# Token lists of a routed expert layer: running ranks and a step function over partitions instead of one-hot products

## The chip, the cores and the metric

The kernel runs on one core of one Trainium2 chip. The metric is the device time of one execution in microseconds; the median over repeated runs counts. TensorE is called PE here, VectorE DVE, ScalarE ACT, GpSimd POOL and SyncE SP.

## What is computed

The reference chains three layers. With `x` of 8 x 3072 x 256:

```python
X = np.fft.fft(np.fft.fft(x, axis=1), axis=2).real      # 24576 tokens of 256
g = X @ w_gate
y = (g / (1 + np.exp(-g)) * (X @ w_val)) @ w_out        # 1536 hidden columns
logits = y @ moe2_w_gate                                # 8 experts
# pairs (token, expert) in falling order of logit: a token takes the first expert
# that isn't full; an expert is full with 24576 / 8 = 3072 tokens
for e in range(8):
    mask = assigned == e
    out[mask] = np.maximum(y[mask] @ w1[e], 0) @ w2[e]  # 1024 hidden columns
```

The order of the pairs matters only through who gets which expert, so the kernel need not sort: it finds the expert that fills next and the logit at which it is full, gives it its tokens, shuts it, and goes on with the rest.

## The kernel before

**Phase 1** (`phase1`, L87 to L707) computes y and the logits. It has 48 tiles of 512 tokens (six to a batch), and 12 steps to a tile, one for 128 hidden columns. In a step PE makes the gate and value products (L385) and, for the step three earlier, the out products (L416), each in three passes over high and low parts. ACT and POOL split the hidden values into `hi` (L691) and `lo` (L692), DVE does the work between. POOL also folds the next batch's x (L120 to L134) and splits the transformed data (L371). What happens beside the steps is put into half steps by hand (`at`, `advance`). At a tile's end `finish` (L418) runs four times: ACT copies 128 rows of y and logits out of the accumulator (L423), POOL copies the eight logits to `Lall` (L424), and SP stores the 256 columns of y to `yscr` in DRAM. A tile's 128 rows are 128 tokens two apart, so the store goes to every second row of `yscr`; two columns of the first tile of a batch need one more small store each (L433).

**Phase 2** (`phase2`, L795 on) has eight rounds, one for each expert, in the order in which they fill.

*Search* (`search`, L841): the best open expert of each token (`choose`, L773: DVE), then eleven steps of three bits each that find the threshold. A step compares all logits with seven edges (L864, DVE), counts by products (L872, PE), picks out the counts (L876 to L880, DVE), sums them over partitions (L884, PE) and derives the next edges (L897 to L927, DVE). Then DVE marks the expert's tokens, and running sums along the 192 columns (L976) with products over the partitions (L982, L983) give each token its place in the list, 0 to 3071. POOL writes the logits of the next round, with the expert shut (`ml`, L964).

*Listing* (`listing`, L1007): place s is held as (s >> 7, s & 127). For 16 columns of tokens at a time DVE makes a one-hot matrix of the low part (`lo`, L1025, 128 x 2048), one of the high part (L1019), and the latter times the two bytes of the token's number (L1022). 192 products (L1014) of `lo[:, :, c]` with 48 columns add up the list, and two DVE operations (L1034, L1036) turn it into row numbers `idx`.

*Experts* (`up` L1087, `down` L1114): six blocks of 512 tokens. POOL gathers rows of y by `idx` with four indirect DMAs (L1062), PE transposes them (L1075), eight `up`s of six products (L1095) and four `down`s of 24 products (L1121) follow, and POOL scatters the result by `idx` (L1130). `split_w` (L1050) splits a quarter of an expert's weights: ACT casts (L1055), POOL subtracts (L1056).

*Order.* The program writes each engine's order out by hand. The first search and the first list run alone. After that the generators `searches` and `lists` run beside the products: `go(time)` (L1173) is called in 32 slots of each block, adds the slot's time to a credit (1.3 at most), and takes one step of the list and one of the search as long as the credit is positive; each step yields its cost in DVE time. A list may begin when its search is through and the expert before the current one is done. If the next list is not ready when an expert's last `up` is issued, slots are called with nothing between them until it is (L1206, L1207).

Of the kernel before, what the change touches and what calls it, by code (L numbers as in the profile page):

```python
# [12 lines left out]
I32 = mybir.dt.int32  # L13
AF = mybir.ActivationFunctionType
# [3 lines left out]
P = 128  # L18
# [39 lines left out]
def _tables():  # L58
    """The constant matrices of the two transforms."""
# [27 lines left out]
def phase1(ctx, tc, io, yscr, Lall, ident, NT, choice=None):  # L87
# [11 lines left out]
    # ---- the tables, and x of a batch  # L99
# [16 lines left out]
    def fold(b, i, xs, eng, tags=(("fa", 1), ("fb", 1))):  # L116
        """The sums and differences over the mirrors of both axes; takes two half steps an operation."""
# [24 lines left out]
    def fold_special(b, eng, tags=(("fa", 1), ("fb", 1))):  # L142
# [7 lines left out]
        # row s=768 of the odd sine transform takes the place of row s=0, which is zero  # L150
# [30 lines left out]
    # the words of a block of weights lie where its split parts come to lie  # L181
# [21 lines left out]
    def fold_w(j, gv, cs, tag, bufs):  # L203
        """Yields between the product and what reads it."""
# [56 lines left out]
    # ---- the column d=128, all batches at once  # L261
# [41 lines left out]
    # ---- the transform over s for a tile of 256 pairs: columns [k=1536-h-2j, j falling | k=2j+h]  # L303
    def fft_mm(pp, z, zsp, h, q, sine):
# [3 lines left out]
        if h == 0:  # L308
# [34 lines left out]
    def fft_half(t, sine, tb, res, bk=("F", 1)):  # L343
        """The cosine or the sine transform of a tile; yields before each part."""
# [3 lines left out]
        # the sine data of even k are those of B-, the cosine data of even k those of B+  # L348
# [25 lines left out]
    # ---- gate and value products, silu, out product  # L374
    order = ((0, 0), (1, 0), (0, 1))  # (weights, data) hi or lo
# [12 lines left out]
    def columns(g):  # L388
        """G = cosine part minus sine part, and their sum, mirrored, for the columns of the negative d."""
# [19 lines left out]
    def out_proj(g):  # L409
# [4 lines left out]
        for u in range(4):  # L414
            for i, (a, d) in enumerate(((0, 0), (0, 1), (1, 0))):  # h, weights
                nc.tensor.matmul(Yp[t][u], h[a][:, u * P : (u + 1) * P], Wo[c // 2][:, c % 2, d, :], start=(c == 0 and i == 0), stop=(c == NF - 1 and i == 2))  # L416

    def finish(t, u):  # L418
        b, hf, q = t // 6, (t // 3) % 2, t % 3
        base = b * S  # L420
# [3 lines left out]
        nc.gpsimd.tensor_copy(Lall[:, 4 * t + u, :], ys[:, D:EXT])  # L424
        # tokens of this column of the tile, by partition
        first = tokens(t, u)
        lo, hi = 0, P
        if hf == 0 and q == 0:
            # k=768 has the place of k=1536, which mini_tile() writes; k=0 is its own mirror
            lo, hi = ((0, P - 1), (0, P), (0, P - 1), (1, P))[u]  # L430
            if u == 0 or u == 3:
                k, r = ((base + 768, P - 1), (base + 2304, 0))[u // 3]
                nc.sync.dma_start(yscr[k : k + 1, :], ys[r : r + 1, 0:D])  # L433
        nc.sync.dma_start(yscr[first + 2 * lo : first + 2 * hi - 1 : 2, :], ys[lo:hi, 0:D])

    # ---- the rows k=1536 of all batches: their own mirrors
    def mini_tile():
        """Products in the second half of a step, what reads them in the first half of the next."""
# [52 lines left out]
        nc.sync.dma_start(yscr[1536 : N : S, :], ys[:, 0:D])  # L491
        nc.sync.dma_start(Lall[P - 1 : P, 2 : 4 * NT : 24, :], ys[:, D:EXT])
# [119 lines left out]
    def prep_block(j):  # L612
        """The last third of the weights during the first steps."""
# [49 lines left out]
    def finale():  # L663
        """The choice among the experts, beside the last products."""
# [45 lines left out]
def tokens(t, u):  # L710
    """The first of the 128 tokens, two apart, of column u of tile t."""
# [7 lines left out]
SHIFTS = tuple(range(29, 1, -3)) + (0,)  # the radix search: three bits at a time, the last time two  # L719
MOST = 1.3  # of the time of the vector engine, as much may be saved up  # L720
# [74 lines left out]
def phase2(ctx, tc, io, yscr, Lall, ident, first, out):  # L795
# [211 lines left out]
    def listing(res, first=False):  # L1007
# [9 lines left out]
        for a in range(0, NCOL, CB):  # L1017
# [9 lines left out]
            if todo:  # L1027
                products(*todo.pop())
# [250 lines left out]
```

## Time and profile before

| | |
|---|---|
| median of 3 runs | 3401.03 us (3399.63 to 3402.3) |
| span of the profiled execution | 3402.1 us, 66033 instructions |
| PE busy | 3243.1 us (95%) |
| DVE busy | 2667.1 us (78%) |
| POOL busy | 1833.1 us (54%) |
| ACT busy | 1559.9 us (46%) |
| mean granted clock of PE | 0.971 |

The page shows one execution; what lies around its span isn't shown apart. Busy times are unions of instructions. Products are pipelined, so a single product's duration holds its latency, and the pace of a row of products is read from their starts. Of a wait for several things the one that came last is named.

### The profile page before, as it was taken

How to read it: one execution, taken by the hardware profiler on the slowest of the kernel's cores; microseconds unless marked ns; L12 is line 12 of the kernel's file. 1: busy time of each engine (PE TensorE's matmuls, PEld its weight loads, DVE VectorE, ACT ScalarE, POOL GpSimd, SP SyncE). 2: the span in 40 equal slices, each digit the busy share in tenths (PEclk: the TensorE clock that was granted, in tenths of full speed). 3: DMA queues.
4: the chain of work that ended last, by engine and by line, in shares of the span. 5: the costliest groups of instructions: out<-in, count | busy, mean ns of one | idle time of the engine just before them, and what ended most of it. 6: DMA issues, size and time to landing. Idle time of an engine off the chain costs nothing.

```text
span 3402.1 us, 66033 instructions
## 1 busy us (share of the span) xinstructions
PE 3243.1 (95%) x25155; PEld 3065.6 (90%) x25155; DVE 2667.1 (78%) x5310; ACT 1559.9 (46%) x3022; POOL 1833.1 (54%) x1916
## 2 busy tenths in 40 slices
PE   5999999999999999999999749999999999999998
PEld 3899999999999999999999638888888888889998
DVE  7899999999999999999988877757666666677221
ACT  3556555655655556555655303232333232323343
POOL 4574664755746648557444344444445454545453
PEclk7999999999999999999999859999999999999999
DMA  5110100101001011010000001111111111111111
GB/s 197 30 36 22 50 23 31 48 17 42 31 29 48 17 31 48 17 42 31 23 17 17 17 31 43 52 41 53 44 57 44 57 45 55 40 60 60 43 47 36
DMA packets 72988, 141.83 MB, mean 42 GB/s; under 512 B 15266, under 2 KB 48978, under 8 KB 70624
## 3 DMA queue, kind: packets, MB, share of 16 engines
q1 hardware_dynamic: 51924, 70.46, 6.4%
q0 software_dynamic: 20736, 67.13, 5.9%
q8 instruction: 199, 3.26, 0.4%
q14 instruction: 117, 0.96, 0.1%
q10 hardware_dynamic: 12, 0.01, 0.0%
HBM read 87.17 MB, written 50.39 MB: 40 GB/s over the span
## 4 chain that ended last, share of the span: by engine, by line
PE 86%; DVE 7%; issue 3%; POOL 2%; ACT 1%; DMA 1%; SPq 0%; ACTq 0%; POOLq 0%; DVEq 0%
PE Y L416 22%; PE B L1121 16%; PE A L1095 14%; PE Q L385 11%; PE Pp L385 10%; PE L L1014 4%; PE F L325 2%; PE F L328 2%; PE C L872 2%; PE A L1075 1%; DVE T L396 1%; DVE lo L1025 1%; POOL lo L692 1%; DVE ise L969 1%; DVE hl L1112 1%
## 5 line engine op out<-in xcount | busy, mean ns | idle before, releaser
L692 POOL TENSOR_TENSOR lo<-hh,hi 128x512 fp32r<-128x512 f32 x576 | 746.0, 1295 | 707.0 <-ACT hi L691 696.0
L416 PE MATMUL Y<-Wo,hi 128*128 128x264 f32 x4608 | 866.8, 285 | 0.0
L416 PEld LDWEIGHTS Y<-Wo,hi 128*128 128x128 f32 x4608 | 710.6, 188 | 0.2 <-ACT hi L691 0.2
L416 PE MATMUL Y<-Wo,lo 128*128 128x264 f32 x2304 | 655.0, 284 | 4.5 <-POOL lo L692 3.5
L396 DVE SCALAR_TENSOR_TENSOR T<-tb,w,Q 128x256 f32<-128x256 f32 x1152 | 500.8, 475 | 118.8 <-ACT qs L685 112.1
L1121 PE MATMUL B<-w,hh 128*128 128x256 f32 x3072 | 584.1, 290 | 0.0
L685 ACT COPY qs<-Q 128x512 f32<-128x512 f32 x576 | 340.0, 590 | 520.6 <-PE Q L385 515.4
L1095 PE MATMUL A<-yh,w 128*128 128x512 f32 x1536 | 498.8, 406 | 15.4 <-DVE hl L1112 15.2
L1130 POOL DMA_INDIRECT out_dram<-ot,idx x192 | 201.3, 1048 | 547.6 <-ACT ot L1128 474.1
L1121 PEld LDWEIGHTS B<-w,hh 128*128 128x128 f32 x3072 | 481.0, 192 | 3.1
L404 DVE TENSOR_TENSOR hh<-sl,G 128x512 f32<-128x512 f32 x576 | 471.9, 819 | 1.3 <-ACT sl L699 1.3
L385 PE MATMUL Q<-xh,W 128*128 128x256 f32 x2304 | 445.8, 286 | 16.4 <-DVE T L396 8.3
L1112 DVE SCALAR_TENSOR_TENSOR hl<-A,hh 128x512 fp32r<-128x512 f32 x384 | 262.5, 686 | 243.5 <-ACT hh L1101 223.1
L416 PEld LDWEIGHTS Y<-Wo,lo 128*128 128x128 f32 x2304 | 434.4, 189 | 6.8 <-POOL lo L692 6.8
L1121 PE MATMUL B<-w,hl 128*128 128x256 f32 x1536 | 435.0, 283 | 2.8 <-DVE hl L1112 2.8
L385 PE MATMUL Pp<-xh,W 128*128 128x256 f32 x2304 | 431.1, 280 | 0.0
L1101 ACT ACTIVATE hh<-A 128x512 fp32r<-128x512 f32 x384 | 229.7, 598 | 405.1 <-PE A L1095 349.3
L397 DVE TENSOR_TENSOR G<-Pp,qs 128x512 f32<-128x512 f32 x576 | 392.2, 681 | 0.0
L691 ACT CAST hi<-hh 128x512 fp32r<-128x512 f32 x576 | 360.5, 626 | 65.8 <-DVE hh L404 62.0
L398 DVE TENSOR_TENSOR G<-T,Pp 128x512 f32<-128x512 f32 x576 | 389.1, 675 | 0.0
L385 PEld LDWEIGHTS Q<-xh,W 128*128 128x128 f32 x2304 | 354.3, 189 | 25.9 <-ACT hi L691 17.4
L699 ACT ACTIVATE sl<-G 128x512 f32<-128x512 f32 x576 | 365.4, 634 | 0.0
(241 smaller groups left out, 5653.7 us busy)
## 6 DMA issues: line engine op xcount, KB each, us to landing
xs<-in_x_dram SPq DMA_DIRECT2D x43, 512.0 KB
yscr<-ys SPq DMA_DIRECT2D x168, 128.0 KB
tb<-tscr SPq DMA_DIRECT2D x48, 128.0 KB
raw<-in_wg_dram SPq DMA_DIRECT2D x6, 512.0 KB
raw<-in_wv_dram SPq DMA_DIRECT2D x6, 512.0 KB
rawWo<-in_wo_dram SPq DMA_DIRECT2D x12, 256.0 KB
yg<-yscr,idx POOLq DMA_INDIRECT x192
out_dram<-ot,idx POOLq DMA_INDIRECT x192
```

Of the source, the lines that this page charges most:

```text
L385: nc.tensor.matmul(pp[:, gv * 256 : gv * 256 + 256], W[:, cs, gv, a, cc : cc + P], RI[t][cs][d], start=(i == 0), stop=(i == 2))
L396: nc.vector.scalar_tensor_tensor(T[:, gv, :], tb, w2[:, gv, c : c + 1], pq[:, gv * 256 : gv * 256 + 256], op0=ALU.mult, op1=ALU.add)
L397: nc.vector.tensor_sub(G[:, 0, :], pp, qs)
L398: nc.vector.tensor_add(rev(G[:, 1, :])[:, :, ::-1], T, rev(pp))
L404: nc.vector.tensor_mul(hh, s["sl"], s["G"][:, :, 256:512])
L416: nc.tensor.matmul(Yp[t][u], h[a][:, u * P : (u + 1) * P], Wo[c // 2][:, c % 2, d, :], start=(c == 0 and i == 0), stop=(c == NF - 1 and i ...
L685: nc.scalar.copy(s["qs"], s["pq"])
L691: nc.scalar.copy(hi, s["hh"])
L692: nc.gpsimd.tensor_sub(lo, s["hh"], hi.bitcast(F32))
L699: nc.scalar.activation(s["sl"], s["G"][:, :, 0:256], AF.Silu)
L1095: nc.tensor.matmul(pa, w[:, a, c : c + P], res["y", i][d][:, k, :], start=(n == 0), stop=(n == 5))
L1121: nc.tensor.matmul(pb[:, 0:D], h[a][:, s * P : (s + 1) * P], w[:, d, (f % 2) * D : (f % 2) * D + D], start=(n == 0), stop=(n == 23))
```

## The change

Three things change. In `finish` the row of y is stored whole, 264 columns, to the rows of `yscr` that the tile's partitions stand for, with the token's number (from a table of 16-bit integers) written over the first logit by POOL. In the search's end the marks are counted by the operations that make them, a running sum over the tokens at the threshold decides which of them still fit, and one more running sum gives `rank`, the number of the expert's tokens in a partition up to a column. The list is then made without one-hot matrices: products with a difference matrix give `x`, for each partition its ranks less those of the partition before, with the partition's start; a step function `on` (is place s at or after the start of partition p, 128 x 3072) summed with `x` over the partitions gives, for each place, the ranks of the partition in which it lies; and counting how many of them are at most the place's offset gives its column. The row number is column x 128 + partition. The scatter uses the token's number out of the gathered row. In the first round `close` (the logits of the next round) and the splits of the first expert's weights change their places in the order.

```diff
     def finish(t, u):
...
-        nc.gpsimd.tensor_copy(Lall[:, 4 * t + u, :], ys[:, D:EXT])
...
-                nc.sync.dma_start(yscr[k : k + 1, :], ys[r : r + 1, 0:D])
-        nc.sync.dma_start(yscr[first + 2 * lo : first + 2 * hi - 1 : 2, :], ys[lo:hi, 0:D])
+        c = 4 * t + u
+        nc.gpsimd.tensor_copy(Lall[:, c, :], ys[:, D:EXT])
+        nc.gpsimd.tensor_copy(ys[:, D : D + 1].bitcast(I32), idt[:, c : c + 1])
+        n = P - 1 if hf == 0 and q == 0 and u == 2 else P
+        nc.sync.dma_start(yscr[c * P : c * P + n, :], ys[0:n, :])
...
     nc.sync.dma_start(t["small"], io["cst"][:, 0:NSMALL])
+    nc.sync.dma_start(t["idt"], io["idt"])
...
+    sio = const.tile([P, CAP], I16, name="sio")
+    nc.sync.dma_start(sio, io["sio"].broadcast_to([P, CAP]))
-    iok = const.tile([P, P, CB], BF16, name="iok")
-    nc.scalar.copy(iok, along(prow, CB))
+    xrow = [const.tile([P, XW], BF16, name=f"xrow{i}") for i in range(2)]
...
-            ml = rp.tile([P, NCOL, E], F32, tag="ml", name="ml")
-            nc.gpsimd.tensor_add(ml, Lall, across(pen, NCOL))
-            res["next"] = ml
+            if ph > 0:
+                close(res)
         yield 1.2
...
         for k, op in enumerate((ALU.is_gt, ALU.is_equal)):
-            nc.vector.scalar_tensor_tensor(sel[:, k, :], m, thr, ise, op, ALU.mult)
-        yield 1.0
-        for k in range(2):
-            nc.vector.tensor_tensor_scan(sc[:, k, :], onesf, sel[:, k, :], 0.0, ALU.mult, ALU.add)
+            nc.vector.scalar_tensor_tensor(sel[:, k, :], m, thr, ise, op, ALU.mult, accum_out=num[:, k : k + 1])
         tot = rp.tile([P, 2], BF16, tag="tot", name="tot")
-        nc.vector.tensor_copy(tot, sc[:, :, NCOL - 1])
-        yield 0.7
-        yield from wait(3)
+        nc.vector.tensor_copy(tot, num)
+        yield 1.3
+        sc = rp.tile([P, NCOL], F32, tag="sc", name="sc")
+        nc.vector.tensor_tensor_scan(sc, onesf, sel[:, 1, :], -float(CAP), ALU.mult, ALU.add)
+        yield 0.4
+        yield from wait(2)
...
+        room = rp.tile([P, 1], F32, tag="room", name="room")
+        nc.vector.tensor_scalar(room, off[:, 1:2], off[:, 2:3], -1.0, ALU.add, ALU.mult)
+        fin = rp.tile([P, NCOL], F32, tag="fin", name="fin")
+        nc.vector.scalar_tensor_tensor(fin, sc, room, sel[:, 1, :], ALU.is_le, ALU.mult)
+        nc.vector.tensor_add(fin, fin, sel[:, 0, :])
+        yield 1.2
+        rank = rp.tile([P, NCOL], BF16, tag="rank", bufs=2, name="rank")
+        nc.vector.tensor_tensor_scan(rank, onesf, fin, 0.0, ALU.mult, ALU.add)
+        res["rank"] = rank
         if ph < E - 1:
-            nc.vector.scalar_tensor_tensor(alive, slot, 0.5, alive, ALU.is_lt, ALU.mult)
+            nc.vector.tensor_sub(alive, alive, fin)
+        yield 0.8
...
+    def listing(ph, res, first=None):
+        rank = res["rank"]
+        pd = bank("R", 1)
+        nc.tensor.matmul(pd[:, NCOL + 2 : NCOL + 3], trib, rank[:, NCOL - 1 : NCOL], start=True, stop=True)
+        nc.tensor.matmul(pd[:, NCOL : NCOL + 1], shiftb, rank[:, NCOL - 1 : NCOL], start=True, stop=True)
+        nc.tensor.matmul(pd[:, 0:NCOL], difb, rank, start=True, stop=True)
         yield 0
+        begin = rp.tile([P, 1], F32, tag="begin", name="begin")
+        nc.vector.tensor_copy(begin, pd[:, NCOL + 2 : NCOL + 3])
+        x = xrow[ph % 2]
+        nc.scalar.copy(x[:, 0 : NCOL + 1], pd[:, 0 : NCOL + 1])
+        yield 0.2
+        on = rp.tile([P, NS, P], BF16, tag="on", name="on")
+        flat = on.rearrange("p n s -> p (n s)")
+        for a in range(0, CAP, 512):
+            nc.vector.tensor_scalar(flat[:, a : a + 512], sio[:, a : a + 512], begin, None, ALU.is_ge)
+            yield 0.3
+        res["idx"] = []
+        for i in range(NS // 2):
+            pl = bank("A", 3) if first else bank("L", 1)
+            v = pl.rearrange("p (a c) -> p a c", a=2)
+            for a in range(2):
+                nc.tensor.matmul(v[:, a, 0:XW], on[:, 2 * i + a, :], x, start=True, stop=True)
+            yield 0
+            j = rp.tile([P, 2], F32, tag="j", bufs=2, name="j")
+            nc.vector.tensor_sub(j, siota[:, 2 * i : 2 * i + 2], v[:, :, NCOL])
+            cc = rp.tile([P, 2], F32, tag="cc", bufs=2, name="cc")
+            for a in range(2):
+                le = rp.tile([P, NCOL], F32, tag="le", bufs=2, name="le")
+                nc.vector.tensor_scalar(le, v[:, a, 0:NCOL], j[:, a : a + 1], None, ALU.is_le, ALU.add, accum_out=cc[:, a : a + 1])
...
+            nc.vector.scalar_tensor_tensor(res["idx"][-1][:, k : k + 2], cc, float(P), v[:, :, NCOL + 1], ALU.mult, ALU.add)
+            if first and i % 2:
+                first(i // 2)
+            yield 1.5
...
     def gather(res, i):
-        yg = work.tile([P, 4, D], F32, tag="yg", bufs=2, name="yg")
+        yg = work.tile([P, 4, EXT], F32, tag="yg", bufs=2, name="yg")
...
+        if k == 1:
+            res["id", i] = work.tile([P, 4], I32, tag="id", bufs=3, name="id")
+            nc.scalar.copy(res["id", i], yg[:, :, D].bitcast(I32))
...
     for _ in search(0, exp[0]):
         pass
-    for j, _ in enumerate(listing(exp[0], True)):
-        if j > 3 and j % 2 and j < 14:
-            split_w(exp[0], 1 + (j > 11))
-    gather(exp[0], 0)
-    for _ in range(3):
+    for _ in range(4):
+        split_w(exp[0], 1)
+
+    def begin(i):
+        if i == 0:
+            gather(exp[0], 0)
+            close(exp[0])
+
+    for _ in listing(0, exp[0], begin):
+        pass
+    for _ in range(4):
         split_w(exp[0], 2)
```

`NS` is 24 (blocks of 128 places) and `XW` is 194. `bank(tag, n)` takes the next of n accumulator banks, so `bank("L", 1)` waits for the readers of the pair before.

## Rows read from the trace of the kernel before

**Rows 1.** The page: the chain that ended last, by engine and by line.

```profile
PE 86%; DVE 7%; issue 3%; POOL 2%; ACT 1%; DMA 1%; SPq 0%; ACTq 0%; POOLq 0%; DVEq 0%
PE Y L416 22%; PE B L1121 16%; PE A L1095 14%; PE Q L385 11%; PE Pp L385 10%; PE L L1014 4%; PE F L325 2%; PE F L328 2%; PE C L872 2%; PE A L1075 1%; DVE T L396 1%; DVE lo L1025 1%; POOL lo L692 1%; DVE ise L969 1%; DVE hl L1112 1%
```

**Rows 2.** Windows by stage: us, busy PE, PEld, DVE, ACT, POOL; clock; DMA.

```profile
60.00:1860.00 1800.00, 1772.88 (x14664) 1750.76 (x14663) 1640.12 (x3076) 1052.02 (x2078) 1102.00 (x1082) 0.99 0.10 31
...
1925.00:2039.00 114.00, 43.62 (x351) 35.13 (x351) 90.98 (x221) 8.81 (x17) 37.83 (x35) 0.51 0.09 31
...
2219.00:3255.00 1036.00, 1019.06 (x7345) 909.64 (x7344) 662.45 (x1486) 337.51 (x625) 492.88 (x570) 0.99 0.15 50
```

**Rows 3.** Windows of expert 1 (list and search beside it) and 6 (list alone).

```profile
2218.00:2394.00 176.00, 172.63 (x1253) 152.93 (x1252) 119.66 (x277) 56.21 (x104) 83.04 (x97) 0.99 0.15 49
...
3095.00:3254.00 159.00, 159.00 (x1107) 146.49 (x1106) 64.36 (x106) 56.18 (x104) 78.73 (x94) 1.00 0.16 54
```

**Rows 4.** Line L1014 alone in the window of expert 1: busy PE, PEld.

```profile
2218.00:2394.00 176.00, 20.81 (x192) 18.26 (x192) 0.99 0.15 49
```

**Rows 5.** Instruction groups by line, whole span: the one-hot matrices on DVE.

```profile
L1025 DVE TENSOR_TENSOR lo<-hlb,iok 128x2048 bf16<-128x2048 bf16 x96 | 141.4, 1473 | 70.6 <-PE L L1014 70.3
...
L1022 DVE TENSOR_TENSOR v<-hi,idb 128x384 bf16<-128x384 bf16 x180 | 57.0, 355 | 3.3
```

**Rows 6.** Timeline around the first list: start us, duration us, instruction.

```profile
1986.51 3.43 POOL L964 TENSOR_TENSOR ml<-Lall,pen 128x1536 f32<-128x1536 f32 x1
...
1989.90 2.18 ACT L1055 CAST w<-w1f 128x512 fp32r<-128x512 f32 x4 [55.51 <-issue]
...
2030.56 0.18 DVE L1036 SCALAR_TENSOR_TENSOR idx<-L,idl 128x24 int32<-128x24 f32 x1
...
2034.81 0.95 POOL L1062 DMA_INDIRECT yg<-yscr,idx  x1 [0.30 <-issue]
...
2037.60 1.33 PE L1075 MATMUL A<-ident,yg 128*128 128x128 f32 x5 [0.74 <-DMA yg<-yscr,idx]
...
2038.75 1.22 PE L1095 MATMUL A<-yh,w 128*128 128x512 f32 x2
```

**Rows 7.** Instruction groups by line: operations like those of a pair, on DVE.

```profile
L995 DVE TENSOR_SCALAR si<-slot 128x192 int32<-128x192 f32 x8 | 2.1, 260 | 0.3
...
L900 DVE DVE_READ_ACCUMULATOR sat<-mx 128x1 f32 x70 | 5.8, 83 | 0.0
```

**Rows 8.** Timeline of PE in expert 1: products of a search step, the next.

```profile
2223.10 0.42 PE L872 MATMUL C<-ge,oh 128*128 128x112 bf16 x5
2223.34 0.70 PE L1095 MATMUL A<-yh,w 128*128 128x512 f32 x2
```

**Rows 9.** Waits of PE in the window of expert 1: total us, times, longest.

```profile
PE A L1095 <- DVE hl L1112: 3.1, 2, 2.8
```

**Rows 10.** Copies to Lall (min/median/max ns); timeline at tile ends; SP's start.

```profile
L424 POOL COPY Lall<-ys x189: 179/190/691, 146.0 to 1925.0; 128x8 f32<-128x8 f32 x189
...
827.16 1.04 POOL L424 COPY Lall<-ys 128x8 f32<-128x8 f32 x4
...
830.12 1.28 POOL L692 TENSOR_TENSOR lo<-hh,hi 128x512 fp32r<-128x512 f32 x1
...
831.45 0.39 PE L416 MATMUL Y<-Wo,lo 128*128 128x264 f32 x1
...
867.94 1.29 POOL L692 TENSOR_TENSOR lo<-hh,hi 128x512 fp32r<-128x512 f32 x1
...
869.52 0.28 PE L416 MATMUL Y<-Wo,lo 128*128 128x264 f32 x1
...
979.41 1.30 POOL L692 TENSOR_TENSOR lo<-hh,hi 128x512 fp32r<-128x512 f32 x1
...
981.70 0.28 PE L416 MATMUL Y<-Wo,lo 128*128 128x264 f32 x1
...
1.20 0.41 SPq L765 DMA_DIRECT2D small<-in_cst_dram  x1
```

More of the change, by code (lines that the diff above doesn't have):

```diff
@@ L490, in mini_tile @@
         nc.vector.tensor_copy(ys, pp[0:B, 0:EXT])
-        nc.sync.dma_start(yscr[1536 : N : S, :], ys[:, 0:D])
-        nc.sync.dma_start(Lall[P - 1 : P, 2 : 4 * NT : 24, :], ys[:, D:EXT])
+        lm = work.tile([B, E], F32, tag="lm", bufs=1, name="lm")
+        nc.vector.tensor_copy(lm, ys[:, D:EXT])
+        nc.vector.tensor_copy(ys[:, D : D + 1].bitcast(I32), idt[0:B, NCOL : NCOL + 1])
+        nc.sync.dma_start(yscr[3 * P - 1 : N : S, :], ys)
+        nc.sync.dma_start(Lall[P - 1 : P, 2 : 4 * NT : 24, :], lm)
     def off_peak(gen, s):
@@ L752, in _route_consts @@
     step = np.concatenate(step).view(np.int32)
-    return cst, np.broadcast_to(step, (P, len(step))).copy()
+    return cst, np.broadcast_to(step, (P, len(step))).copy(), idt, np.arange(CAP, dtype=np.int16).reshape(1, CAP)
 NSMALL = 2 * E + 16
@@ L829, in phase2 @@
     nc.gpsimd.memset(pen, 0.0)
-    idb = const.tile([P, 2, NCOL], BF16, name="idb")
-    nc.scalar.copy(idb.rearrange("p a c -> p (a c)"), ids)
-    trib = const.tile([P, P], BF16, name="trib")
-    nc.scalar.copy(trib, tri)
-    iok = const.tile([P, P, CB], BF16, name="iok")
-    nc.scalar.copy(iok, along(prow, CB))
+    trib, shiftb, difb = (const.tile([P, P], BF16, name=n) for n in ("trib", "shiftb", "difb"))
+    for a, b in ((trib, tri), (shiftb, shift), (difb, dif)):
+        nc.scalar.copy(a, b)
+    xrow = [const.tile([P, XW], BF16, name=f"xrow{i}") for i in range(2)]
+    for a in xrow:
+        nc.scalar.copy(a[:, XW - 1 : XW], after)
     def wait(n):
@@ L986, in search @@
         nc.vector.tensor_copy(off, po[:, 0:4])
-        nc.vector.tensor_add(off[:, 1:2], off[:, 1:2], off[:, 2:3])
-        for k in range(2):
-            nc.vector.scalar_tensor_tensor(sc[:, k, :], sc[:, k, :], off[:, k : k + 1], sel[:, k, :], ALU.add, ALU.mult)
-        yield 1.0
-        slot = rp.tile([P, NCOL], F32, tag="slot", name="slot")
-        nc.vector.tensor_add(slot, sc[:, 0, :], sc[:, 1, :])
-        nc.vector.scalar_tensor_tensor(slot, slot, CAP + 0.5, slot, ALU.is_lt, ALU.mult)
@@ L1003, in search @@
-        yield 0.9
-        if ph < E - 1:
-            nc.vector.scalar_tensor_tensor(alive, slot, 0.5, alive, ALU.is_lt, ALU.mult)
-    def listing(res, first=False):
-        hlb = res["hlb"]
-        pl = bank("L", 1)
-        def products(a, lo, v):
-            for c in range(CB):
-                nc.tensor.matmul(pl[:, 0:48], lo[:, :, c], v[:, :, :, c], start=(a + c == 0), stop=(a + c == NCOL - 1))
-        todo = []
-        for a in range(0, NCOL, CB):
-            hi = rp.tile([P, 24, CB], BF16, tag="hi24", bufs=2, name="hi24")
-            nc.vector.tensor_tensor(hi, across(hlb[:, 0, a : a + CB], 24), iok[:, 0:24, :], ALU.is_equal)
-            v = rp.tile([P, 2, 24, CB], BF16, tag="v", bufs=3, name="v")
-            for k in range(2):
-                (nc.gpsimd if first and k else nc.vector).tensor_mul(v[:, k], hi, across(idb[:, k, a : a + CB], 24))
-            yield 0.9
-            lo = rp.tile([P, P, CB], BF16, tag="lo", bufs=2, name="lo")
-            nc.vector.tensor_tensor(lo, across(hlb[:, 1, a : a + CB], P), iok, ALU.is_equal)
-            yield 1.1
-            if todo:
-                products(*todo.pop())
-            todo.append((a, lo, v))
-        yield from wait(2)
-        products(*todo.pop())
-        yield 0
-        idl = rp.tile([P, 24], F32, tag="idl", name="idl")
-        nc.vector.tensor_copy(idl, pl[:, 24:48])
-        idx = rp.tile([P, 24], I32, tag="idx", bufs=2, name="idx")
-        nc.vector.scalar_tensor_tensor(idx, pl[:, 0:24], 256.0, idl, ALU.mult, ALU.add)
-        res["idx"] = idx
@@ L1130, in down @@
         st = nc.gpsimd.indirect_dma_start(
[L1131 removed]
+            out=out, out_offset=bass.IndirectOffsetOnAxis(ap=res["id", i][:, s : s + 1].bitcast(mybir.dt.uint32), axis=0), in_=ot, in_offset=None
         )
@@ L1150, in lists @@
                 yield 0
-            yield from listing(exp[ph])
+            yield from listing(ph, exp[ph])
             ready.append(ph)
```

54 lines of the change are left out of this document (25 added, 29 removed).

## The prediction

> **What bounds the kernel now.** Read the page first: PE is busy for 95% of the span (the small table above), and in the chain of waits it carries 86%, the products of the lists (L1014) alone 4% [rows 1]. An average over stages proves little, so the windows come next [rows 2]. The stage of the transforms and the gated layer (60 to 1860 us) keeps PE busy for 1772.88 of 1800 us; the seven expert intervals from 2219 us on keep it busy for 1019.06 of 1036. Only from 1925 to 2039 us, where the first search and the first list run with nothing beside them, PE works 43.62 of 114 us and DVE 90.98: DVE and waiting set the time there, and the granted clock is 0.51 of full, so PE is at the lower of its two levels (1.2 GHz) nearly throughout. So each PE microsecond removed beside the experts should shorten the run, each DVE microsecond removed in the gap as well, and nothing else does unless it makes PE wait. DVE is no rival of PE beside the experts as it stands: 119.66 of 176 us in one expert's window [rows 3].
>
> **Lists beside the experts.** One listing runs in each of the windows of the first seven experts. Its 192 products load 128 weight columns each and move only 48, and the loads set their pace: 18.26 us of loads, 0.095 us each [rows 4]. The window whose expert has a list but no search beside it is all PE [rows 3], so the 18.26 us leave whole. In their place come, per list, 24 products (two for each of 12 pairs of 128 places) that move 194 columns, one of 192 and two of one column. Five products of 112 columns with loads of their own start 0.24 us ahead of what follows them, 0.048 us each [rows 8]: they run at the pace of their columns, 0.43 ns a column. Their weights lie side by side as those of the new step function do, while L1014 reads every sixteenth element. So I take 194 columns at 0.083 us: 24 x 0.083 + 0.1 = 2.1 us, and 0.1 us for each of 13 places where PE changes over from other products, 3.4 us. Gain per list 18.26 - 3.4 = 14.9 us, times 7 = 104 us. Bounds: were each of the 24 as slow as an L1014 product (0.095) and each pair to cost 0.3 us of waiting, 18.26 - (2.4 + 1.3 + 3.6) = 11.0, so 77 us; were the change-overs free, 18.26 - 2.1, so 113 us. The Trainium skill ("TensorE: Matmul & The Clock Gate", section "LDWEIGHTS (loading the stationary operand)") puts a load at its columns over 1.2, in ns, so 107 ns for 128. By that rule the 24 products would cost 2.6 us instead of 2.0 and the sum would come out some 4 us higher; the measured 0.048 us of a product with its load is below the rule, and the measurement decides.
>
> DVE's share of a list falls too. Now its two largest groups take 141.4 and 57.0 us over eight lists [rows 5], 25 us each. After: a pair is two counts over 192 columns (0.26 us each by the nearest operation, and 0.083 to read the sum [rows 7]) and two operations on two columns of some 0.2, about 1.1 us with issue; 12 pairs are 13 us, six operations of 512 columns 0.3 to 0.6 us each are 2 to 4. So 8 to 10 us or more go from 119.66 and the interval shrinks to about 161: DVE's share stays at 0.68. PE waits 3.1 us for `hl` in such a window now [rows 9]; with the operations of L1025 (1.47 us on average [rows 5]) gone that may go (7 x 3.1 = 22 us more), or grow by as much. I take nothing and keep 22 us each way for the range's ends.
>
> **The first list.** It ends with idx at 2030.56, the last gather issues at 2034.81, its rows are in by 2037.60, and the first expert starts at 2038.75 [rows 6]. After the change the chain is another one. The four splits of w1 are now issued ahead of the list, so ACT's copy of the row `x` stands behind their casts, which end at 1989.90 + 2.18 = 1992.08 (the weights land then, by a load that the change doesn't move; the search's tail, shorter and without the 3.43 us of POOL's `ml` in its way [rows 6], lies under that wait). `x` is there at about 1992.5, and the 12 pairs at 1.14 us end at 2006.5; splitting the first block takes about 1 us more: the expert starts at 2007.5, 31 us earlier. The gather doesn't decide: its places are known after two pairs (1995.2), POOL has done the four splits of w1 by 1995.7 (1.3 us each, as `lo` of the same size [rows 10]), four issues take 5 us, and the last rows come 2.8 us after their issue [rows 6], at 2003.5. `close` (3.43 us) and the splits of w2 follow on POOL under the first products. Bounds: with 0.9 us a pair the gather decides, 2004.6, 34 us; with 1.5 us a pair and 4 us of blocking by POOL, 2016, 22 us.
>
> **The end of expert 0.** Counting the planner's costs slot by slot (the listing yields 24.0 now and 20.0 after, but over 32 steps instead of 27), the first list is not ready when the last up products are issued; now four empty slots follow, afterwards eight, with three pairs in them and the start of a search step. PE needs DVE's reads before each next pair, so it stands for about two pairs and one search operation: 2 x 1.14 + 2 x 0.8 + 0.8 = 5 us. Bounds 0 and 9. For the later experts the count has no empty slot in either version.
>
> **The rows of y.** Per tile POOL gets four copies of one column more. The four copies that stand there take 1.04 us; one copy lasts 0.69 at most against a median of 0.19, beside a DVE operation on two tiles, so one of the four is held up and the others, which overlap, take (1.04 - 0.69) / 3 = 0.12 us of POOL's queue each [rows 10]. Four more are 0.5 us, or 1.05 if one is held up. Behind them waits `lo`, and behind that PE. In one tile of a batch `lo` ends 0.05 us ahead of the product that reads it (830.12 + 1.28 against 831.45), in two 0.3 (867.94 + 1.29 against 869.52), in three 1.0 (979.41 + 1.30 against 981.70) [rows 10]. So PE loses 0.45 + 2 x 0.2 = 0.9 us a batch, in seven of them 6 us; bounds 0 and (1.0 + 2 x 0.75 + 3 x 0.05) x 7 = 19. The stores of y stay 192 and lose 16 small ones; each now waits for POOL's copy as well as ACT's, about 1 us later, and behind it in SP's queue stand loads of x and of `tb` that are wanted a tile later, so that is hidden; SP has one table more ahead of the first weights, by the issue of another small table 0.4 us [rows 10]. The copies of the number on ACT, the new constants and the 32 bytes more in a row are hidden: ACT is busy 56.21 of 176 us [rows 3], the scatters wait for that copy, which is made a block ahead of them, and a gather has a block's products as cover (176 / 6 = 29 us [rows 3]); without it, PE would wait for each.
>
> **The sum.** 3402.1 - 104 - 31 + 5 + 6 + 0.4 = 3278.5 against the profiled span. The runs' median, 3401.03, lies 1.1 us under that span; taking that off as well gives **3277.4 us**, 3.6% less.
>
> **Rivals.** *Waiting pair by pair (slower).* PE takes its work in order, the list beside an expert has one bank, and each pair's products wait until DVE has read the pair before. If DVE runs behind, PE stands at every one of 84 pairs. It decides against the change from 123.6 / 84 = 1.47 us a pair on; at 2 us a pair the time is 3277 + 168 = 3445. For it: a pair is 1.1 us of DVE, and a column of up products leaves it little room. Against it: the planner books 1.5 us for a pair and keeps at least one slot between, and PE waits only 3.1 us in a whole window although DVE's operations in the list are longer now [rows 5, 9]. Chance 3%.
>
> *DVE becomes the bound.* Freed PE time runs into the search's and `hl`'s operations, and half of the 104 us comes back: 3329. Against it, DVE's share of a window doesn't rise, as worked out above. Chance 9%.
>
> *The lock in phase 1.* Each tile end meets DVE's two-tile operation once more: 19 us instead of 6, 3290. The third copy's hold-up speaks for it, the 1.0 us of room in three tiles of six against. The Trainium skill ("SBUF — State Buffer", section "Who interferes with whom") says that a DVE instruction with two SBUF inputs and a GpSimd instruction that reads SBUF block each other for a whole instruction; by that rule one of the four new copies is the most that is likely to be caught in a step, and these 1.05 us are the price. Chance 15%.
>
> *More goes than counted.* PE's waits for `hl` vanish with the long operations of L1025: 3277 - 22 = 3255. Chance 13%.
>
> *The change doesn't bring what it says:* something that I don't see holds each list to the old pace: 3370, the first list's 31 us alone. Chance 2%.
>
> **The numbers.** The forecast's own chance is 58%. Its range, 3260 to 3305, comes from the bounds of the terms; the two rivals that lie beside it at 3255 and 3290 stretch it to 3250 to 3318, and I leave out the last ones and most of the second, some 15%. A measurement of this kernel tells about 0.2% (7 us) from no change. Of the cases only the first rival ends slower; between it and a gain lies little: faster 0.95, same 0.02, slower 0.03.
>
> **What would show it.** In the profile after: no L1014; a list of 27 products per expert with some 3 us on PE; expert intervals of about 160 us instead of 175; the first up product near 2007 plus the loss of phase 1; ACT's copy of `x` behind the casts of w1; PE waiting on POOL's `lo` for some 6 us before 1860; and one PE gap of 5 us at the end of expert 0. PE waits of over 1 us at the pairs, or intervals above 168 us, would make it wrong.

## The result, and the profile after

The changed kernel takes 3295.94 us (median of 4 runs, 3293.48 to 3296.86) against 3400.94 for the kernel before (4 runs, 3399.63 to 3402.3): ratio 0.9692, 95% interval 0.9678 to 0.9706. The forecast was 3277.4, its range 3250 to 3318. The profiled execution has a span of 3291.7 us (3293.48 with what lies around it). It splits at two starts that any trace shows, the end of the last Y product and the first up product:

| us | before | after | difference | forecast |
|---|---|---|---|---|
| until the last Y product ends | 1925.6 | 1957.0 | +31.4 | +6.4 |
| from there to the first up product | 113.1 | 80.3 | -32.8 | -31 |
| the eight experts | 1354.1 | 1245.1 | -109.1 | -99 |
| after the last down product | 9.3 | 9.3 | 0 | 0 |

The gap and the experts gave 141.9 us, 12 more than forecast, and 25 us more than forecast were paid back in the first stage, which the change barely touches.

The first view after is the windows by stage (us, busy PE, PEld, DVE, ACT, POOL; clock; DMA), to be held against [rows 2].

```profile
60.00:1890.00 1830.00, 1778.72 (x14652) 1751.03 (x14651) 1664.94 (x3076) 1052.86 (x2078) 1130.97 (x1264) 0.99 0.10 30
1957.00:2037.00 80.00, 27.37 (x181) 18.39 (x180) 63.09 (x255) 6.89 (x19) 17.69 (x22) 0.52 0.15 53
2204.00:3245.00 1041.00, 1013.26 (x6968) 902.66 (x6967) 602.49 (x1648) 381.41 (x742) 541.61 (x634) 0.99 0.17 55
```

In the first window PE is idle for 51 us where it was idle for 27; in the gap DVE has 63 us of work where it had 91; beside the experts PE is idle a little more than before, 28 of 1041 us. The waits of PE until 1960 us (in total, times, longest) say who it waits for in the first stage:

```profile
PE Y L417 <- POOL lo L691: 28.9, 25, 1.6
PE Q L386 <- DVE T L397: 8.1, 20, 1.5
```

The same two before:

```profile
PE Y L416 <- POOL lo L692: 3.5, 4, 1.3
PE Q L385 <- DVE T L396: 8.3, 20, 1.5
```

The timeline of one tile end shows how (start, duration, instruction; compare 827.16 and 830.12 in [rows 10]):

```profile
840.16 0.20 POOL L425 COPY Lall<-ys 128x8 f32<-128x8 f32 x1
840.42 0.65 POOL L427 CAST ys<-idt 128x1 int32<-128x1 int16 x1
841.01 0.18 POOL L425 COPY Lall<-ys 128x8 f32<-128x8 f32 x1
841.26 0.19 POOL L427 CAST ys<-idt 128x1 int32<-128x1 int16 x1
841.38 0.19 POOL L425 COPY Lall<-ys 128x8 f32<-128x8 f32 x1
...
842.02 0.19 POOL L427 CAST ys<-idt 128x1 int32<-128x1 int16 x1
842.16 0.74 POOL L372 TENSOR_TENSOR xl<-ab,xh 128x256 fp32r<-128x256 f32 x1
842.85 1.29 POOL L121 TENSOR_TENSOR fa<-xs 128x512 f32<-128x512 f32 x1
843.29 1.40 DVE L405 TENSOR_TENSOR hh<-sl,G 128x512 f32<-128x512 f32 x1
844.10 1.73 POOL L691 TENSOR_TENSOR lo<-hh,hi 128x512 fp32r<-128x512 f32 x1
845.88 0.39 PE L417 MATMUL Y<-Wo,lo 128*128 128x264 f32 x1 [1.57 <-POOL lo L691]
```

Four copies and four casts, one after the other, hold POOL for 842.16 - 840.16 = 2.0 us; the four copies alone took 1.04. `lo` comes 1.0 us later, and now it meets L405 on DVE, and lasts 1.73 us instead of 1.28. PE stands for 1.57 us. At each of the 48 tile ends one of POOL's short instructions is held up, before a copy and now a cast; the means (us in all, mean ns of one) of the copies before, and of the copies and casts after, show it, as one that isn't held takes 0.18 to 0.20 us:

```profile
L424 POOL COPY Lall<-ys 128x8 f32<-128x8 f32 x192 | 49.9, 307 | 1.3 <-ACT ys L423 1.3
L425 POOL COPY Lall<-ys 128x8 f32<-128x8 f32 x192 | 36.2, 188 | 0.9 <-ACT ys L423 0.9
L427 POOL CAST ys<-idt 128x1 int32<-128x1 int16 x192 | 58.6, 305 | 12.5
```

The gap: ACT and PE around the first list in the timeline (compare [rows 6]).

```profile
2021.44 2.18 ACT L1068 CAST w<-w1f 128x512 fp32r<-128x512 f32 x4 [57.60 <-DVE on L1029]
2023.53 0.31 ACT L1024 CAST xrow<-R 128x193 bf16<-128x193 f32 x1
2023.89 1.13 PE L1036 MATMUL A<-xrow,on 128*128 128x194 bf16 x6 [4.92 <-ACT xrow L1024]
...
2033.02 0.51 PE L1036 MATMUL A<-xrow,on 128*128 128x194 bf16 x2 [0.55 <-DVE idx L1047]
2034.08 0.50 PE L1036 MATMUL A<-xrow,on 128*128 128x194 bf16 x2 [0.55 <-DVE idx L1047]
2035.18 2.19 PE L1088 MATMUL A<-ident,yg 128*128 128x128 f32 x8 [0.60 <-DVE j L1039]
2037.35 1.19 PE L1111 MATMUL A<-yh,w 128*128 128x512 f32 x2
```

This is the chain of the forecast: the casts of w1, the row `x`, and pairs 1.06 us apart. Beside the experts, the 24 products of the pairs in the window of expert 1 (busy PE, PEld; compare [rows 4]), and PE's waits from the first up product on:

```profile
2203.00:2369.00 166.00, 4.26 (x24) 1.40 (x24) 0.97 0.16 52
```

```profile
PE C L879 <- DVE ge L871: 9.7, 5, 2.1
PE L L1036 <- DVE idx L1047: 9.6, 7, 3.0
PE B L1137 <- DVE hl L1128: 7.5, 3, 3.1
PE R L988 <- DVE tot L981: 4.5, 2, 2.3
PE A L1111 <- DVE hl L1128: 3.1, 1, 3.1
```

By the starts of the records a list's products took 18.1 us of PE before and take 1.7 now; for seven lists that is 115 us. Here `ge` are the search's comparisons, `tot` its counts of the marks, `idx` the row numbers of a pair, and `hl` the low part of the hidden layer. The waits in this stage sum to 34.4 us; before they were 21.3, most of it in these three:

```profile
PE A L1095 <- DVE hl L1112: 15.2, 10, 2.8
PE B L1121 <- DVE hl L1112: 2.8, 1, 2.8
PE A L1075 <- DMA yg<-yscr,idx: 2.2, 2, 1.2
```

The experts' intervals are 165.5, 165.9, 161.8, 160.3, 162.8, 148.6, 142.3 and 138.0 us (before 180.0, 175.8, 175.5, 174.3, 175.8, 174.8, 158.8 and 139.0): the last search now ends earlier in expert 5 (its last counting product at 2886 us, 32 us into it; before at 3002, 82 us into it), so expert 5 gains most, 26.2 us, and expert 6 16.5. The last one has no list, and is 1.0 us shorter all the same.

### The profile page after: what moved, and what is told of

Same layout as the page of the kernel before. It is cut to its first block, busy times and chain, and to the rows that moved or that the text cites. A ratio compares the mean times of both kernels' runs of the same rounds, so it can differ in the third digit from the quotient of the medians.

```text
span 3291.7 us, 64128 instructions
## 1 busy us (share of the span) xinstructions
PE 3112.7 (95%) x23835; PEld 2936.8 (89%) x23835; DVE 2575.4 (78%) x5524; ACT 1565.5 (48%) x3080; POOL 1843.8 (56%) x2096
## 3 DMA queue, kind: packets, MB, share of 16 engines
q14 instruction: 123, 1.01, 0.1%
## 4 chain that ended last, share of the span: by engine, by line
PE 81%; issue 6%; POOL 5%; DVE 5%; ACT 1%; DMA 1%; SPq 0%; POOLq 0%; ACTq 0%; DVEq 0%
PE Y L417 22%; PE B L1137 16%; PE A L1111 14%; PE Q L386 11%; PE Pp L386 10%; PE F L326 2%; PE F L329 2%; POOL lo L691 2%; PE C L879 1%; PE A L1088 1%; POOL ys L427 1%; DVE T L397 1%; POOL xl L372 1%; DVE ge L871 1%; ACT qs L684 0%
## 5 line engine op out<-in xcount | busy, mean ns | idle before, releaser
L691 POOL TENSOR_TENSOR lo<-hh,hi 128x512 fp32r<-128x512 f32 x576 | 757.7, 1316 | 694.8 <-ACT hi L690 685.2
L405 DVE TENSOR_TENSOR hh<-sl,G 128x512 f32<-128x512 f32 x576 | 501.3, 870 | 1.3 <-ACT sl L698 1.3
L1146 POOL DMA_INDIRECT out_dram<-ot,id x192 | 198.8, 1036 | 457.2 <-ACT ot L1144 354.3
```

The source lines that it names most:

```text
L405: nc.vector.tensor_mul(hh, s["sl"], s["G"][:, :, 256:512])
L691: nc.gpsimd.tensor_sub(lo, s["hh"], hi.bitcast(F32))
```

## The experiments

**Is it POOL's casts?** The kernel before, with the casts alone added:

```diff
         nc.gpsimd.tensor_copy(Lall[:, 4 * t + u, :], ys[:, D:EXT])
+        nc.gpsimd.tensor_copy(ys[:, D : D + 1].bitcast(I32), idt[:, 4 * t + u : 4 * t + u + 1])
```

> The kernel before, with only GpSimd's four conversions of token numbers added to each tile's rows of y (its stores still take 256 columns to scattered token rows, so the added numbers are not used). Theory P (the 31 us that phase 1 lost come from these conversions, one after the other with the copies of the logits on GpSimd): the last Y product ends at 1950 to 1960 us instead of 1925.6, the wait of the Y products for the low part grows by 1.3 us at three tile ends of a batch, and the whole takes 3427 to 3435 us. Rival W (the loss comes from the stores of whole rows of 264 columns in tile order): phase 1 stays within 3 us of 1925.6 and the whole within 4 us of 3401.

Measured: 3432.91 us (one execution), 32.5 above the kernel before on the same chip; the last Y product ends at 1958.2. The wait is the same one, as often and as long, and the gap and the experts stay as before (113.3 and 1350.4 us):

```profile
PE Y L417 <- POOL lo L694: 29.1, 25, 1.6
```

Set against the kernel before, step by step, all of it falls into one step, that with the second group of the next tile's out products (+32.4 us over 48 tiles), 10.3, 9.3 and 9.2 of it at the ends of three of a batch's six tiles, and some 1 us in each of the others. Theory P stands; that the wider stores in tile order cost nothing that shows is seen in the next experiment, which has them.

**Where the casts stand.** The changed kernel, with the casts (and the stores, which need them) issued behind the next step's `lo`:

```diff
         nc.gpsimd.tensor_copy(Lall[:, c, :], ys[:, D:EXT])
-
+        held.append((t, u, ys))
+
+    held = []
+
+    def store(t, u, ys):
...
         nc.gpsimd.tensor_copy(ys[:, D : D + 1].bitcast(I32), idt[:, c : c + 1])
...
             s["h"] = (hi, lo)
+        while held:
+            store(*held.pop(0))
```

> The changed kernel with GpSimd's four conversions of a tile, and the four stores behind them, issued after the subtraction that makes the low part of the next step instead of ahead of it; the four copies of the logits stay where they are. As many instructions on GpSimd as in the changed kernel. If their place ahead of the low part is what costs (the Y products wait for that subtraction), phase 1's last Y product ends at 1925 to 1931 and the whole takes 3264 to 3271 us. If GpSimd's sum of work in a tile is what costs, wherever it stands, phase 1 stays within 5 us of 1957 and the whole within 5 us of 3296.

Measured: 3262.09 us (one execution), the last Y product at 1925.9, the wait for `lo` back at 3.5 us in 4 times. The same tile end on POOL:

```profile
827.20 1.06 POOL L425 COPY Lall<-ys 128x8 f32<-128x8 f32 x4
828.21 0.74 POOL L372 TENSOR_TENSOR xl<-ab,xh 128x256 fp32r<-128x256 f32 x1
828.91 1.30 POOL L121 TENSOR_TENSOR fa<-xs 128x512 f32<-128x512 f32 x1
830.15 1.30 POOL L697 TENSOR_TENSOR lo<-hh,hi 128x512 fp32r<-128x512 f32 x1
831.39 1.01 POOL L433 CAST ys<-idt 128x1 int32<-128x1 int16 x4
```

POOL does as many instructions, and phase 1 loses nothing. The place ahead of `lo` was the price, not POOL's sum of work. In a row, the four casts take 1.01 us; between the copies they added 1.0 as well, but there the fold and `xl` and then `lo` stood behind them.

**Two instructions instead of eight.** One buffer for the four columns of a tile:

```diff
+        ys = work.tile([P, 4, EXT], F32, tag="ys", bufs=1, name="ys")
+        for u in range(4):
+            nc.scalar.copy(ys[:, u, :], Yp[t][u])
...
+        nc.gpsimd.tensor_copy(Lall[:, c : c + 4, :], ys[:, :, D:EXT])
+        nc.gpsimd.tensor_copy(ys[:, :, D].bitcast(I32), idt[:, c : c + 4])
...
```

> The changed kernel with the four columns of a tile in one buffer: four copies by ScalarE as now, then one copy of the logits of all four and one conversion of four numbers on GpSimd (two instructions for eight), then the four stores. Theory P: GpSimd has some 0.6 to 0.8 us at a tile end, less than the 1.0 us of the kernel before; phase 1's last Y product ends at 1915 to 1928, the whole takes 3255 to 3268 us. Rival W: 1957 and 3296. A third, that the stores of a tile now leave later and the next tile's copies wait for the one buffer: a wait of ScalarE for the stores at the tile ends, and more than 3296.

Measured: 3264.82 us (3262.61 to 3265.97), ratio to the kernel before 0.9599 (0.9583 to 0.9615); last Y product at 1926.6. At a tile end POOL has

```profile
904.47 0.55 POOL L425 COPY Lall<-ys 128x32 f32<-128x32 f32 x1 [0.33 <-ACT ys L423]
905.08 0.19 POOL L426 CAST ys<-idt 128x4 int32<-128x4 int16 x1
905.22 0.73 POOL L135 TENSOR_TENSOR z<-fb 128x256 f32<-128x256 f32 x1
```

0.75 us from the first start to the next instruction, but the copy starts only when ACT has made all four parts. It is as good as the kernel before, not better; the lower end of the expectation was not reached.

**The number written by ACT**, into a column of its own (265 to a row):

```diff
...
-        nc.gpsimd.tensor_copy(ys[:, D : D + 1].bitcast(I32), idt[:, c : c + 1])
+        nc.scalar.copy(ys[:, EXT:ROW].bitcast(I32), idt[:, c : c + 1])
...
```

> The changed kernel with the token's number put by ScalarE into a column of its own (265 columns a row), so GpSimd has only the four copies of the logits of a tile, as before the change; the stores are as wide and in the same order. Theory P: phase 1 gets back 25 to 31 us, its last Y product ends at 1926 to 1932, the whole takes 3265 to 3271 us; ScalarE's four short copies (0.2 us each) may cost up to 1 us a tile at the same three tile ends of a batch, which would leave 3285. Rival W: phase 1 stays at 1957, the whole at 3296.

Measured: 3286.33 us (3285.20 to 3288.63). The wait for `lo` is back at 3.6 us, as theory P has it, but only 21 of the 31 us return (last Y product at 1935.9): ACT's copy of `qs` now comes later, and the first step of each tile is 0.25 us longer, 12 us in all. And the experts take 1258.8 us, 13.7 more, which no theory expected. That the time comes near the 3285 us which the expectation named is chance: ACT's copies cost 0.25 us at every tile and not 1 us at three ends of a batch, and the rest came from the experts. In the last expert, where nothing is searched or listed, the up products are slower (PE by line in that expert, here and then in the changed kernel; busy us, mean ns of one):

```profile
L1112 PE MATMUL A<-yh,w 128*128 128x512 f32 x192 | 60.6, 397 | 0.0
```

```profile
L1111 PE MATMUL A<-yh,w 128*128 128x512 f32 x191 | 59.0, 390 | 0.0
```

They start 233.4 ns apart instead of 227.1. Their instructions are the same ones; what differs, counted from the program, is that the longer rows move the buffers behind them in a partition by 64 bytes.

**Where buffers lie.** That raised the question whether part of the experts' gain is of this kind. The changed kernel, with the hidden layer's buffers moved by 32 bytes:

```diff
         transpose(exp[0], 0, k, True)
+    work.tile([P, 8], F32, tag="pad", bufs=1, name="pad")
```

> The changed kernel with 32 unused bytes ahead of the buffers of the hidden layer, so that these lie at 32 modulo 128 bytes in a partition, as in the kernel before, and no longer at 0. Theory S (a part of what the experts gained is not the lists: the down products start every 119.5 ns instead of 121.3 in the last expert, in which no list is made, because the buffers moved): the mean pitch of the down products in the last expert goes back to 121.0 to 121.5 ns, the last expert to 139.0 us, and the whole to 3302 to 3306 us. Rival: the pitch has another cause (the changed order of the work, the clock); it stays at 119.5, the last expert at 138.0 and the whole at 3296.

Measured: 3298.76 us (3295.24 to 3301.23), ratio 0.9696 (0.9679 to 0.9712): by the time alone not told apart from the changed kernel. In the trace the last expert takes 138.8 us instead of 138.0, the down products 120.9 ns instead of 119.5 (121.3 before). So moving buffers alone changes the pace by about 1%, and most of the last expert's 1.0 us is of that kind. How much it is over all eight stays open: they take 1252.2 us in this trace, 7.1 more than in the changed kernel's, but kernels that leave these buffers in place differ by 3 us there too (1244.8 in a4_casts_after_lo, 1248.0 in a3_one_cast_a_tile), and the medians lie only 2.8 us apart, less than expected.

Then all the experts' buffers at 0 modulo 128 bytes, by the program's count, in the kernel with one cast a tile:

```diff
...
+    wp.tile([P, 24], F32, tag="pad", bufs=1, name="pad")
...
+    work.tile([P, 8], F32, tag="pad", bufs=1, name="pad")
```

> The kernel with one conversion a tile (3264.8 us) with unused bytes put so that the weights, the tokens and the hidden layer of the experts all lie at 0 modulo 128 bytes. Theory S: the pitch of the up products goes below 227 ns or that of the down products below 119.5 in the last expert, the whole to 3250 to 3262 us. Rival: both stay within 0.3 ns, and the whole within 2 us of 3264.8.

Measured: 3267.38 us (3264.39 to 3269.50), down products 120.9 ns, up 227.1: not better. That addresses matter is shown; by what rule stays open, and 0 modulo 128 is not it.

**The first list.** The prediction's chain can be cut: `x` ahead of the splits of w1, which then follow the first gather.

```diff
-    for _ in range(4):
-        split_w(exp[0], 1)
     def begin(i):
         if i == 0:
             gather(exp[0], 0)
+            for _ in range(4):
+                split_w(exp[0], 1)
             close(exp[0])
```

> The changed kernel with the four parts of w1 for the first expert split after the first gather, instead of ahead of the list. If the chain of the first list is as the prediction had it (ScalarE's copy of the ranks' row stands behind a copy of w1, then twelve pairs), the first pair starts 1.5 to 4 us earlier and the first product of expert 0 comes 1 to 4 us earlier, the whole at 3292 to 3295; if the gather decides, or the splits then decide the first product, the first product stays within 0.5 us of 2037.35 minus the start of the search or comes later.

Measured: 3295.51 us (one execution). The gap is 76.9 us instead of 80.3, so the chain was read rightly; but expert 0 takes 169.1 us instead of 165.5, and nothing is left. The theory was that the next search now starts no earlier, as its input `ml` (L1009) stood behind the splits. So, with the splits left behind the gather, `ml` was issued ahead of the list, in the kernel with the casts behind `lo`:

```diff
+    close(exp[0])
...
     def begin(i):
...
-            close(exp[0])
...
```

> The kernel with the conversions behind the low part (3262.1 us), with the first list's ranks' row ahead of the splits of w1 as in c1_x_row_first, but with the sum that the next search starts from (ml, 3.5 us on GpSimd) issued ahead of the list instead of behind the gather. Theory: c1_x_row_first brought the first product of expert 0 3.4 us nearer, and lost it again because the next search, whose chain bounds the experts with a search, did not start any earlier. Then here expert 0 is not longer than 166 us and the whole comes to 3255 to 3260 us. Rival: expert 0 was longer because the parts of w1 came late or for another cause; expert 0 again takes 168 us or more, and the whole 3261 to 3264 us.

Measured: 3262.67 us (3261.75 to 3263.40). Expert 0 takes 164.5 us, as the theory had it, but the gap is 80.3 again. DVE, while POOL does `ml` (1985.99, 3.43 us):

```profile
1985.53 4.12 DVE L1008 TENSOR_TENSOR fin<-fin,sel 128x192 f32<-128x192 f32 x1
```

Without `ml` beside it this takes 0.36 us. Last, `ml` behind the gather and the splits behind `ml`, and the base again on the same chip:

```diff
...
             gather(exp[0], 0)
             close(exp[0])
+            for _ in range(4):
+                split_w(exp[0], 1)
```

> The kernel with the conversions behind the low part (3262.1 us), with the splits of w1 behind the first gather as in c1_x_row_first, but behind ml too, so that ml follows the gather at once. In c3_next_input_first ml stood beside VectorE's sum of two SBUF operands (fin), which took 4.12 us instead of 0.36; beside the pairs, which read PSUM, it has cost nothing visible. Theory: the first product of expert 0 comes 76.9 us after the last Y product instead of 80.3, and expert 0 stays within 163 to 166 us, since its search starts no later; the whole 3256 to 3260 us. Rival: w1's parts come late behind ml and the first up products wait for them; expert 0 is 168 us or more and the whole 3261 to 3264.

> The kernel of a4_casts_after_lo with more rounds: 3260 to 3264 us, the base to which c4_ml_then_splits is compared on the same chip.

Measured: 3263.86 us (3263.26 to 3264.54) against 3264.05 (3261.07 to 3264.60), no difference. The gap is 76.6 us, expert 0 takes 169.0 again. The theory of the late search falls: `ml` was early. DVE's queue at the start of expert 0, here and then in the base:

```profile
2004.83 5.12 DVE L796 TENSOR_TENSOR eq<-ml,m 128x768 f32<-128x768 f32 x1
2009.88 1.28 DVE L1139 SCALAR_TENSOR_TENSOR hl<-A,hh 128x512 fp32r<-128x512 f32 x2
```

```profile
2009.00 1.54 DVE L796 TENSOR_TENSOR eq<-ml,m 128x768 f32<-128x768 f32 x1
2010.46 0.68 DVE L1139 SCALAR_TENSOR_TENSOR hl<-A,hh 128x512 fp32r<-128x512 f32 x1
```

`eq` reads two SBUF operands, takes 0.95 us as the median of its line, and here stands until POOL has done four splits of w2 in a row (2004.15 to 2009.14); `hl` stands behind it in DVE's queue, and the fourth group of up products behind `hl`, 2.1 us late. In c1_x_row_first the same `eq` took 4.77 us. The other 1.4 us of the loss fall some 100 us into expert 0, where the granted clock is 0.50 (1.2 GHz) from 2102.1 to 2108.9 us, twice as long as in the base (2106.1 to 2109.5); what lengthened it was not tried.

**Pairs closer or further apart** in the schedule:

```diff
-            yield 1.5
+            yield 1.1
```

The base is the kernel with one cast a tile.

> The kernel with one conversion a tile (3264.8 us) with a pair of the list entered at 1.1 in the schedule instead of 1.5 (a pair took 1.06 us where it ran alone). The prediction had it that the waits at the pairs come where the schedule runs out of products (three empty slots at the end of expert 0) and not where a pair stands between products. By that, the lists and the searches are done some slots earlier, the wait of the pairs' products for the indices falls from 10.0 us by 3 to 6, and the experts take 1242 to 1250 us. Rival (each pair makes TensorE wait when VectorE's work is packed closer): the waits for the indices and for ge grow by over 6 us together, and the experts take 1254 us or more.

Measured: 3275.21 us, experts 1257.7 (1248.0 at 1.5). PE's waits beside the experts (the base has 10.0, 9.7 and 3.1 us of `idx`, `ge` and up products' `hl`):

```profile
PE C L877 <- DVE ge L869: 14.1, 8, 2.2
PE L L1034 <- DVE idx L1045: 9.5, 8, 4.5
PE A L1109 <- DVE hl L1126: 8.5, 3, 6.7
```

> The kernel with the conversions behind the low part (3262.1 us), with a pair of the list entered at 1.9 in the schedule instead of 1.5. At 1.1 the experts took 9.7 us longer. If that came from VectorE's work being packed closer than it can be done, 1.9 takes 2 to 8 us off the waits of experts 1 to 5 (ge, idx, hl) and adds slots: the experts at 1238 to 1250 us. If the lists' slots are what runs short (the list must be done before its expert begins), the waits at the ends of the experts grow and the experts take over 1250 us.

Measured, with 1.9 and the casts behind `lo`: 3275.81 us, experts 1258.5 (1244.8 at 1.5), waits of PE:

```profile
PE C L890 <- DVE ge L882: 12.7, 14, 2.1
PE R L999 <- DVE tot L992: 12.4, 5, 3.6
```

Both are some 10 to 14 us slower (one execution each). At 1.1 expert 0, which ends in empty slots, takes 159.6 us instead of 165.5, and experts 1 to 5 lose: the waits for `ge` and the up products' waits for `hl` grow by 9.8 us together where DVE's work is packed closer, while those for `idx` do not grow (9.5 and 10.0). So this is the rival in which freed PE time runs into DVE's search and `hl`, more than the one in which PE waits pair by pair, and it lies one step away from the chosen number. At 1.9 the waits that grow are the search's, for `tot` in the middle of an expert and for `ge` near its start and end. All waits there sum to 42 us where they were 35 at 1.5; the other half of the 13.7 us was not followed up.

## Why the prediction was right, and where a step failed

- **Lists beside the experts** (-104): 18.1 us a list went and 1.7 came, 16.4 for each of seven instead of 14.9; the change-overs at 0.1 us each did not show. Of these 115 us PE's waits took 13 back, a term that the prediction put at nothing, with 22 us each way in the range. Besides, the granted clock is at its lower level (0.50) for 31 us of the experts, before for 20, which is up to 5 us at half pace and no term of the sum. What remains to the measured 109.1 is 7 to 12 us; eight times the 1.0 us of the last expert is 8. That this remainder is the pace of the moved buffers in all of them is argued, shown only for the last. The rule that was weighed (the Trainium skill, "TensorE: Matmul & The Clock Gate", section "LDWEIGHTS (loading the stationary operand)": 107 ns for 128 columns) would have made the 24 products 2.6 us, as an estimate; the trace has 1.7 with their loads, so it does not hold here.
- **The first list** (-31): -32.8 by the chain that was named, pairs at 1.06 us instead of 1.14, and the first block's transposes (2035.18) ran under the last pair instead of behind it. The gather did not decide, as said.
- **The end of expert 0** (+5): the place was right, three pairs in empty slots, with waits of 1.35, 1.04 and 1.10 us, 3.5 in all. What follows was no part of the term: the granted clock is 0.50 from 2185.6 to 2192.4 us and the down products start 0.21 us apart instead of 0.12, some 2.5 us of half pace. The kernel before lost time there as well, 2.2 us in two waits for the gather and 0.50 of the clock from 2209.8 to 2213.2 us. So the change costs some 2 to 3 us there, and that waits and half pace together come near 5 is chance.
- **The rows of y** (+6, bounds 0 and 19): this is the term that failed, at 31 us. The prediction took 0.5 us of POOL for four casts, 0.12 each, from copies that overlap in a row; alternating with the copies they take 1.0. A cast starts 0.25 us after the copy of the same buffer (841.01, 841.26) and the next copy 0.12 later (841.38); that the shared buffer is the reason is argued. The hold-up that the prediction weighed for the casts added nothing, as one instruction of a tile end was held up before too. The upper bound had 1.05 us for the casts; beyond it, `lo`, 1.0 us later, ran into DVE's L405 and took 0.45 more at three tile ends of seven batches, 9 us in all. So the three tiles with 0.05, 0.3 and 0.3 us of room lost 1.42, 1.29 and 1.28 us a batch instead of 0.45, 0.2 and 0.2, and the three with 1.0 us some 0.15 each instead of nothing. The rooms themselves were read rightly, and the loss came at just those tiles. Had the term been 31, the sum would have been 3302, 7 us above the measurement.
- **The sum**: the misses of +25 us in the first stage and -12 behind it cancel in part, so the distance of 18.5 us to the forecast is smaller than the worst term's. Of it 5 us are no term at all: the prediction took 1.1 us off the profiled span to reach the median, and the new median lies 4.2 us above its profiled span. Two small readings in the prediction are off without moving its range: 0.45 + 2 x 0.2 is 0.85, and the rival at 3290 lies inside 3260 to 3305 and not beside it.
- **The rivals**: the lock in phase 1 came true in part, at `lo` and not at the casts, and with the casts' own 1.0 us the loss went beyond its 19 us. DVE did not become the bound at this setting, but PE's waits for it grew by 13 us although DVE's share of a window stayed at 0.68. The prediction's own sign of being wrong, waits of over 1 us at the pairs, did come: besides the three at the end of expert 0 there is one of 3.0 us in expert 1 and one of 2.7 in expert 4. With the smaller ones they cost 9.6 us in all.

## What to carry to other kernels

Before adding small instructions to an engine that "has room", look at what stands behind them in its queue and at the slack of each place: 192 casts on POOL cost nothing behind `lo` and 31 us ahead of it. Moving the casts by one subtraction takes the kernel to 3264.05 us, ratio 0.9594 (0.9581 to 0.9607) to the kernel before, and that is the version to keep. Time won on a chain of DVE and POOL can be lost at the next place where both read SBUF, so follow it to the end of the stage before booking it.

## What was not expected of the hardware

- A DVE instruction with two SBUF operands can wait for a whole run of POOL instructions and not only for one: `eq` took 5.12 us until four subtractions in a row were done, and 4.77 in c1_x_row_first. It need not: at the tile end shown above L405 (843.29 to 844.69 us) got its turn between POOL's fold and `lo`, and `lo` stood instead. What decides between the two is not shown. Counts that read PSUM (L1043, 0.42 us) kept their 1.06 us a pair beside `ml`. That the former contend and the latter don't agrees with the Trainium skill ("SBUF — State Buffer", section "Who interferes with whom"), by which a DVE instruction with at most one SBUF input, outside the modes that use both ports, does not contend with GpSimd, while one with two contends with a GpSimd instruction that reads SBUF.
- The same matmuls ran 1 to 3% slower or faster in kernels whose buffers lie 32 or 64 bytes apart: up products 227.1 or 233.4 ns apart, down products 119.5, 120.9 or 121.3.
